# Reordering the segment loop of a recurrent attention kernel on TensorE: half-0 scores ahead of V, the last V bank between the PV halves, one Wo chunk behind PV half 1

## The chip, the cores and the metric

The kernel runs on 1 core of a Trainium2 chip. The metric is the device time of one execution in microseconds (us), as the median of several executions. "Timed" means these executions; "traced" means the one execution of a kernel that the profile was taken from. Engines are named as in the profile: PE is TensorE's matmuls, PEld its weight loads, DVE is VectorE, ACT is ScalarE, POOL is GpSimd.

## The reference

The work is a gated sum of two attention blocks. Block B (a linear-memory attention over four long segments) is the first quarter of the kernel's time and is not touched. Block A is a recurrence over 64 short segments, and it is what this case is about:

```python
for s in range(n_seg):                         # 64 segments of 32 tokens, 8 memory tokens
    h = jnp.concatenate([mem, xs], axis=1)     # 40 rows, 512 wide
    q = jnp.einsum('btd,dhe->bhte', h, Wq)     # 32 heads of 128
    k = jnp.einsum('btd,dhe->bhte', h, Wk)
    v = jnp.einsum('btd,dhe->bhte', h, Wv)
    scores = jnp.einsum('bhqe,bhke->bhqk', q, k) * scale
    p = _softmax(jnp.where(mask[None, None], scores, -1000000000.0), axis=-1)
    o = jnp.einsum('bhqk,bhke->bhqe', p, v)
    o = jnp.einsum('bhte,hed->btd', o, Wo)
    mem = o[:, :M, :].copy()                   # the next segment needs this
    outs.append(o[:, M:, :])
```

Each segment's memory rows come out of the segment before, so segments run strictly one after the other. Inside a segment, V needs only `h`; it does not depend on the softmax.

## The kernel before

A small planner records operations per engine in program order and puts semaphore waits between engines from read and write sets. In the traces of before and after, PE, ACT and DVE run their operations in that order in all 61 segments that start after 380 us (but for one matmul record of PE in before, which stands ahead of three of the scores), so **the order of the Python calls is the order of each engine's queue**. Heads are handled in two halves (0 and 1) for everything from the scores on. Per segment:

```python
def vproj(j):                      # one PSUM bank of V: 8 matmuls 128x512, then its eviction
    P.op("pe", f_v, ..., name="v%d_%d" % (s, j))
    if j in (1, 2):
        P.op("act", ...)           # banks 1 and 2 are evicted by ACT
    else:
        P.op("dve", ...)           # banks 0 and 3 by DVE
# ... cut: scores (32 small matmuls), softmax_exp (exp on ACT, mask on DVE) ...
def softmax_norm(i):
    P.op("pe", ...)                # row sums: one matmul with ones
    P.op("act", ... ACT.Ln)        # ln of the sums
    P.op("act", ... ACT.Exp, scale=-1.0)   # exp(-ln) = inverse
    P.op("dve", ... ALU.mult)      # normalised P
def pv(i):                         # 16 matmuls, then evicted by ACT (one group) and DVE (the other)
    ...
def wo(i, c):                      # 16 weight-load and matmul pairs 128x40: half i, output chunk c
    ...

kq("K", 0); kq("K", 1); kq("K", 2)     # 128 pairs 128x40 (cut: output tail of every fourth segment)
kq("Q", 0); kq("Q", 1); kq("Q", 2)     # 128 pairs 128x40
vproj(0)
scores(0, 16)
scores(16, 32)
softmax_exp(0)
softmax_exp(1)
vproj(1)
softmax_norm(0)
vproj(2)
softmax_norm(1)
vproj(3)
pv(0)
pv(1)
for c in range(C):                     # C = 4
    wo(0, c)
wo(1, 0); wo(1, 1)                     # cut: memory and output copies (tail)
wo(1, 2); wo(1, 3)
```

The softmax here doesn't subtract the row's maximum and nothing guards it: scores larger than these inputs give would overflow.

## Time and profile before

| | before |
|---|---|
| timed, median of 4 (range) | 1468.8 us (1467.2 to 1472.1) |
| traced | 1482.0 us, span 1480.2 us |
| segment phase, first to last Wo stage, 63 periods | 1108.4 us, 17.59 us each |
| shortest period without / with an output tail | 16.50 / 17.58 us |
| stretches at half clock in that phase | 35, together 120 us |

A segment's *period* here is the distance between the starts of two Wo stages in the timeline. Every fourth segment carries an output tail, about 1.1 us. The shortest period of each kind I call the *floor*: it is what the schedule costs when nothing disturbs it.

The page of before: the busy times of the engines, the granted PE clock in 40 slices (9 is 90% or more of full), and who is on the chain of work that ended last.

```profile
PE 1251.3 (85%) x35605; PEld 980.8 (66%) x35653; DVE 621.3 (42%) x1542; ACT 579.6 (39%) x1280; POOL 106.1 (7%) x212
...
PEclk8978697677999999999999999998999999999998
...
PE 57%; ACT 12%; DVE 5%; issue 2%; SPq 1%; DMA 1%
```

PE is the busiest engine, but 17% of the chain runs on ACT and DVE. The chain of waits of before through one softmax (start us, length us, what) shows where:

```profile
727.24 0.60 ACT V_sb L865
727.84 0.34 ACT R_sb L902
...
730.01 0.49 DVE Pn_sb L906
730.50 0.61 DVE V_sb L868
731.11 0.14 issue
731.25 0.37 PE pb L918 x16
```

ACT evicts V bank 1 (L865) *before* it takes the Ln of half 0 (L902), the same again for half 1 (left out), and PV half 1 (L918) starts only when DVE has evicted V bank 3 (L868). The view of waits of PE over the segment phase, from 380 us on (us in total, times, longest), puts a number on it:

```profile
PE pb L918 <- DVE V_sb L868: 82.9, 63, 1.3
PE pb L840 <- issue: 10.1, 24, 0.8
PE pb L943 <- issue: 4.1, 8, 1.2
```

PE stands idle 1.31 us per segment in front of PV half 1. I call this **the hole**.

What a hole does later is seen in stretches of 1 us of the same trace. The first column is the stretch, then its length, busy time of PE, PEld, DVE, ACT and POOL with instruction counts; the third number from the end is the granted clock.

```profile
1100.00:1101.00 1.00, 0.17 (x14) 0.06 (x6) 0.75 (x2) 0.65 (x2) 0.29 (x1) 1.00 0.00 0
...
1102.00:1103.00 1.00, 1.00 (x44) 1.00 (x43) 0.39 (x1) 0.34 (x1) 0.00 (x0) 1.00 0.00 0
1103.00:1104.00 1.00, 1.00 (x39) 1.00 (x35) 0.00 (x0) 0.00 (x0) 0.00 (x0) 0.60 0.09 16
1104.00:1105.00 1.00, 1.00 (x36) 1.00 (x33) 0.12 (x2) 0.00 (x0) 0.00 (x0) 0.50 0.00 0
```

The hole is at 1100.2 to 1101.5; from 1103.2 on PE runs at half clock for 3.41 us, and successive matmuls of Wo and K start 33 ns apart in place of 25.4, although PE is "100% busy" in both. At half clock these pairs thus run at about three quarters of their rate (25.4 of 33 ns), not at half. A Wo stage that holds a whole such stretch takes 4.2 us in place of 3.4. This is why PE's busy share alone would have hidden the second cost.

The third thing to see is the "issue" gap. The timeline of PE of before (start us, length us, engine, line, operation, count, and in brackets the idle time and what ended it):

```profile
1421.47 0.76 PE L943 MATMUL pb<-OT_sb,Wo_sb 128*128 128x40 bf16 x24 [0.73 <-issue]
...
1425.38 0.77 PE L840 MATMUL pb<-hT,Wk_sb 128*128 128x40 bf16 x24 [0.55 <-issue]
...
1429.13 0.77 PE L840 MATMUL pb<-hT,Wq_sb 128*128 128x40 bf16 x24 [0.38 <-issue]
```

Each time exactly 24 of a group's 128 matmuls are left: the gaps lie 128 weight-load and matmul pairs, 256 instructions, apart.

### The profile page before, as it was taken

The numbers are of one execution on the slowest core, as the hardware profiler recorded it, in microseconds if no ns is written. First come the engines' busy times: TensorE is split into PE (matmuls) and PEld (weight loads), VectorE is DVE, ScalarE is ACT, GpSimd is POOL, SyncE is SP. The second block draws the span as 40 slices with busy tenths as digits, with TensorE's granted clock in tenths as the row PEclk, the third lists the DMA queues.
The fourth block names the chain that finished last, engine by engine and source line by source line (L and its number), as shares of the span: only waits on it lengthen the run. The fifth ranks groups of instructions, "written<-read, shape, count | busy, mean of one in ns | idle before, by whom it ended". The sixth has DMA issues, their size and how long they took to land.

```text
span 1480.2 us, 75277 instructions
## 1 busy us (share of the span) xinstructions
PE 1251.3 (85%) x35605; PEld 980.8 (66%) x35653; DVE 621.3 (42%) x1542; ACT 579.6 (39%) x1280; POOL 106.1 (7%) x212
## 2 busy tenths in 40 slices
PE   4767676766999899998998998989998998999988
PEld 3544444445777777776777767777777776777776
DVE  3547676552333334333333434333333343433333
ACT  4757475662333333333333333333333333333333
POOL 1322132220000000000000000000000000000000
PEclk8978697677999999999999999998999999999998
DMA  8000000006000000000000000000000000000000
GB/s 341 3 2 3 2 2 2 2 2 229 4 7 4 7 4 7 4 7 4 7 7 4 7 4 7 4 8 4 7 4 8 4 7 4 7 4 7 4 7 7
DMA packets 12891, 27.90 MB, mean 19 GB/s; under 512 B 800, under 2 KB 11048, under 8 KB 11048
## 3 DMA queue, kind: packets, MB, share of 16 engines
q1 hardware_dynamic: 12584, 23.09, 4.3%
q8 instruction: 280, 4.59, 1.3%
q14 instruction: 27, 0.22, 0.0%
HBM read 20.99 MB, written 2.10 MB: 16 GB/s over the span
## 4 chain that ended last, share of the span: by engine, by line
PE 57%; ACT 12%; DVE 5%; issue 2%; SPq 1%; DMA 1%
PE pb L840 28%; PE pb L943 17%; PE pb L859 8%; ACT V_sb L865 5%; ACT R_sb L904 4%; ACT R_sb L902 3%; DVE V_sb L868 3%; DVE Pn_sb L906 2%; PE pb L885 2%; PE pb L918 2%; PE pb L1008 1%; DMA Wo_sb<-in_A_Wo_dram 1%; SPq L310 1%; PE pb L1016 0%; SPq L304 0%
## 5 line engine op out<-in xcount | busy, mean ns | idle before, releaser
L859 PE MATMUL pb<-Wv_sb,hT 128*40 128x512 bf16 x2048 | 268.2, 383 | 2.0 <-DMA Wv_sb<-in_A_Wv_dram 2.0
L943 PE MATMUL pb<-OT_sb,Wo_sb 128*128 128x40 bf16 x8192 | 244.6, 188 | 9.4 <-issue 4.1
L847 ACT ACTIVATE KT_sb<-pb 128x480 bf16<-128x480 f32 (+1 forms) x192 | 100.9, 526 | 383.4 <-PE pb L840 383.4
L943 PEld LDWEIGHTS pb<-OT_sb,Wo_sb 128*128 128x128 bf16 x8192 | 238.3, 101 | 15.3 <-issue 8.7
L850 DVE CAST QT_sb<-pb 128x480 bf16<-128x480 f32 (+1 forms) x192 | 115.6, 602 | 298.1 <-PE pb L840 291.0
L840 PE MATMUL pb<-hT,Wk_sb 128*128 128x40 bf16 x8192 | 224.5, 181 | 7.8 <-issue 5.0
L840 PE MATMUL pb<-hT,Wq_sb 128*128 128x40 bf16 x8192 | 220.2, 180 | 7.5 <-issue 6.8
L840 PEld LDWEIGHTS pb<-hT,Wk_sb 128*128 128x128 bf16 x8192 | 217.4, 97 | 9.2 <-issue 9.0
L840 PEld LDWEIGHTS pb<-hT,Wq_sb 128*128 128x128 bf16 x8192 | 212.3, 96 | 10.0 <-issue 9.5
L593 ACT ACTIVATE PT_g<-pb 128x512 bf16<-128x512 f32 (+1 forms) x384 | 170.2, 529 | 59.7 <-PE pb L584 58.9
L892 ACT ACTIVATE P_sb<-pb 104x320 bf16<-104x320 f32 x128 | 49.0, 434 | 271.5 <-PE pb L885 271.5
L859 PEld LDWEIGHTS pb<-Wv_sb,hT 128*40 128x40 bf16 x2048 | 85.2, 99 | 81.2 <-issue 3.5
L906 DVE TENSOR_TENSOR Pn_sb<-P_sb,R_sb 104x320 bf16<-104x320 bf16 x128 | 63.0, 492 | 140.6 <-ACT R_sb L904 140.6
L918 PE MATMUL pb<-Pn_sb,V_sb 40*128 40x40 bf16 x2048 | 47.6, 178 | 84.1 <-DVE V_sb L868 84.1
L918 PEld LDWEIGHTS pb<-Pn_sb,V_sb 40*128 40x128 bf16 x2048 | 36.0, 93 | 116.0 <-ACT OT_sb L927 89.0
L988 DVE CAST hT<-pb 128x16 bf16<-128x16 f32 x126 | 22.0, 174 | 199.5 <-PE pb L943 199.5
L868 DVE CAST V_sb<-pb 104x512 bf16<-104x512 f32 x128 | 88.0, 687 | 33.5 <-PE pb L859 33.5
L599 POOL TENSOR_SCALAR_AFFINE_SELECT PT_g<-PT_g 128x512 bf16<-128x512 bf16 x128 | 82.3, 643 | 241.9 <-ACT PT_g L593 239.7
L799 POOL COPY hT<-xT 128x128 bf16<-128x128 bf16 x64 | 19.0, 298 | 1077.6 <-PE pb L859 1060.3
L584 PE MATMUL pb<-QTg,KTg 16*128 16x128 bf16 x1280 | 43.1, 245 | 52.8 <-ACT PT_g L593 49.6
L927 ACT ACTIVATE OT_sb<-pb 128x320 bf16<-128x320 f32 x128 | 56.0, 437 | 79.8 <-PE pb L918 79.7
L865 ACT ACTIVATE V_sb<-pb 104x512 bf16<-104x512 f32 x128 | 75.3, 588 | 17.5 <-PE pb L859 17.4
(92 smaller groups left out, 1026.2 us busy)
## 6 DMA issues: line engine op xcount, KB each, us to landing
Wk_sb<-in_A_Wk_dram SPq DMA_DIRECT2D x4, 1024.0 KB, 11.6
Wq_sb<-in_A_Wq_dram SPq DMA_DIRECT2D x4, 1024.0 KB, 20.8
Wv_sb<-in_A_Wv_dram SPq DMA_DIRECT2D x4, 1024.0 KB, 9.2
Wo_sb<-in_A_Wo_dram SPq DMA_DIRECT2D x4, 1024.0 KB, 14.3
x_sb<-in_A_x_dram SPq DMA_DIRECT2D x4, 512.0 KB, 5.6
out_dram<-fin SPq DMA_DIRECT2D x16, 128.0 KB, 1.9
wqN_sb<-in_B_wq_dram SPq DMA_DIRECT2D x1, 512.0 KB, 7.3
wkN_sb<-in_B_wk_dram SPq DMA_DIRECT2D x1, 512.0 KB, 8.4
```

Source lines behind the costliest of these rows:

```text
L593: P.op("act", (lambda j=j: (lambda a: a.activation(ptb[:, j, 128 * n0:128 * (n0 + len(wv))], pb[j][:, 0:128 * len(wv)], ACT.Exp, scale=SCA ...
L599: P.op("gp", (lambda n=n: (lambda gq: gq.affine_select(ptb[:, :, 128 * n:128 * (n + 1)], ptb[:, :, 128 * n:128 * (n + 1)], [[0, 4], [1, 128]],
L840: ins = pe.matmul(pb[bnk][:, (p - h0) * L:(p - h0 + 1) * L], wsb[:, c, h * E:(h + 1) * E], hTc[:, c, :], start=(c == 0 and (p == h0 or not ...
L847: P.op("act", lambda a: a.activation(dst[:, h0 * L:h1 * L], pb[bnk][:, 0:(h1 - h0) * L], ACT.Copy), reads=[rbank[bnk]], writes=[rd], name= ...
L850: P.op("dve", lambda dv: dv.tensor_copy(dst[:, h0 * L:h1 * L], pb[bnk][:, 0:(h1 - h0) * L]), reads=[rbank[bnk]], writes=[rd], name="Qev%d_ ...
L859: ins = pe.matmul(pb[j][64 * g2:64 * g2 + L, 0:512], hTc[:, c, :], Wv_sb[:, c, n0:n0 + 512], start=(c == 0), stop=(c == C - 1))
L865: P.op("act", lambda a: a.activation(V_sb[0:NP, 512 * j:512 * (j + 1)], pb[j][0:NP, 0:512], ACT.Copy), reads=[rbank[j]], writes=[rv], name ...
L868: P.op("dve", lambda dv: dv.tensor_copy(V_sb[0:NP, 512 * j:512 * (j + 1)], pb[j][0:NP, 0:512]), reads=[rbank[j]], writes=[rv], name="vev%d ...
L904: P.op("act", lambda a: a.activation(R_sb[0:NP, i * W:(i + 1) * W], R_sb[0:NP, i * W:(i + 1) * W], ACT.Exp, scale=-1.0), reads=[rr], write ...
L906: P.op("dve", lambda dv: dv.tensor_tensor(Pn_sb[0:NP, i * W:(i + 1) * W], P_sb[0:NP, i * W:(i + 1) * W], R_sb[0:NP, i * W:(i + 1) * W], AL ...
L918: ins = pe.matmul(pb[2 * i + g2][:, (t % HB_) * L:(t % HB_ + 1) * L], V_sb[p0:p0 + L, t * E:(t + 1) * E], Pn_sb[p0:p0 + L, t * L:(t + 1) * L],
L943: ins = pe.matmul(pb[bk][:, (c % 2) * L:(c % 2 + 1) * L], Wo_sb[:, h, c * 128:(c + 1) * 128], OT_sb[:, h * L:(h + 1) * L], start=(first an ...
```

## The change

The intent: bring the softmax of half 0 forward so that V banks 0 and 1 run under it; let ACT take Ln and inverse ahead of its V eviction; and fill the time before PV half 1 with work that does not need it (V bank 3 and three of the four Wo chunks of half 0). One Wo chunk stays behind PV half 1 to cover the eviction of its result. No arithmetic changes.

```diff
-    vproj(0)
     scores(0, 16)
+    softmax_exp(0)
+    v_mm(0)
+    v_ev(0)
     scores(16, 32)
-    softmax_exp(0)
     softmax_exp(1)
-    vproj(1)
-    softmax_norm(0)
-    vproj(2)
-    softmax_norm(1)
-    vproj(3)
+    softmax_sum(0)
+    softmax_ln(0)          # Ln, inverse (ACT); for half 0 also the normalise (DVE)
+    v_mm(1)
+    v_ev(1)
+    softmax_sum(1)
+    softmax_ln(1)
+    v_mm(2)
+    v_ev(2)
     pv(0)
+    v_mm(3)
+    softmax_nrm(1)
+    v_ev(3)
+    for c in range(3):
+        wo(0, c)
     pv(1)
-    for c in range(C):
-        wo(0, c)
+    wo(0, 3)
     wo(1, 0)
     wo(1, 1)
```

(`vproj` is split into `v_mm` on PE and `v_ev`, its eviction, and `softmax_norm` into `softmax_sum`, `softmax_ln` and `softmax_nrm`, with unchanged bodies.)

More of the change, by code (lines that the diff above doesn't have):

```diff
@@ L851, in kq, with v_mm @@
                  reads=[rbank[bnk]], writes=[rd], name="Qev%d_%d" % (s, b))
-    def vproj(j):
+    def v_mm(j):
         def f_v(pe):
@@ L862, in vproj, with v_ev @@
         P.op("pe", f_v, reads=[rx] + rm + [Rs("Wv")], writes=[rbank[j]], name="v%d_%d" % (s, j))
+    def v_ev(j):
         rv = Rs("V_sb%d" % j)
@@ L896, in softmax_exp, with softmax_sum, softmax_ln @@
              reads=[rp, Rs("amask")], writes=[rp], name="msk%d_%d" % (s, i))
-    def softmax_norm(i):
-        rp, rr, rn = Rs("P_sb%d" % i), Rs("R_sb%d" % i), Rs("Pn_sb%d" % i)
+    def softmax_sum(i):
+        rp = Rs("P_sb%d" % i)
         P.op("pe", lambda pe: pe.matmul(pb[4 + i][:, 0:W], onesg[0:NP, :], P_sb[0:NP, i * W:(i + 1) * W], start=True, stop=True),
              reads=[rp, Rs("onesg")], writes=[rbank[4 + i]], name="sum%d_%d" % (s, i))
+    def softmax_ln(i):
+        rr = Rs("R_sb%d" % i)
         P.op("act", lambda a: a.activation(R_sb[0:NP, i * W:(i + 1) * W], pb[4 + i][0:NP, 0:W], ACT.Ln),
@@ L905, in softmax_norm, with softmax_nrm @@
              reads=[rr], writes=[rr], name="rex%d_%d" % (s, i))
+        if i == 0:
+            softmax_nrm(0)
+    def softmax_nrm(i):
+        rp, rr, rn = Rs("P_sb%d" % i), Rs("R_sb%d" % i), Rs("Pn_sb%d" % i)
         P.op("dve", lambda dv: dv.tensor_tensor(Pn_sb[0:NP, i * W:(i + 1) * W], P_sb[0:NP, i * W:(i + 1) * W],
```

## The prediction

> **What bounds it now.** The 64 recurrent segments take about 1110 of the 1480 us of the profiled span (first to last Wo stage in the timeline), about 17.3 us each. PE is busy for 85% of the span on the page, DVE 42%, ACT 39%. The chain of waits leaves PE only in the softmax, for ACT and DVE. In the view of waits PE waits most before the second PV half, for the DVE eviction of V bank 3: 80.2 us in 61 waits, 1.31 us per segment.
>
> A second cost hangs on it. In 1 us windows the segment phase shows about 37 stretches at granted clock 0.50, each about 3.41 us, 126 us in all, always behind the hole. A Wo stage that carries one takes 4.2 us in place of 3.41, so each costs about 0.8 us, 29 us in all. [...] all stretches fall on one 3.41 us grid, whose phase against the hole decides.
>
> Third, PE has gaps released by "issue" inside the long Wo-K-Q run: 32 in the segment phase, 14 us, nearly all in segments at full clock (about 0.37 us each between 566 and 696 us).
>
> **What the change does.** The same matmuls and evictions are reordered, none added. Half-0 scores (0.2 us) run first, so the exp and mask of half 0 run under V bank 0 (0.97 us). ACT gets half 0's Ln and inverse ahead of the V bank 1 eviction. V bank 3 (0.98 us) goes behind PV half 0, Wo chunks 0-2 of half 0 (48 matmuls at 25.4 ns, 1.22 us) ahead of PV half 1, chunk 3 (0.41 us) behind it.
>
> Walking the segment with the trace's durations (exp 0.43, Ln 0.46, inverse 0.47, V eviction 0.58 on ACT and 0.68 on DVE, normalise 0.49, PV eviction 0.44/0.49, hand-over 0.1-0.14 us): PV half 0 finds its operands ready; ACT's half-0 PV eviction ends just as V bank 3 leaves PE, so Wo waits 0-0.2; V bank 3 is evicted about 0.3 us before PV half 1 needs it, so the 1.31 us wait goes; Wo of half 1 waits about 0.22 us for the PV evictions, which chunk 3 (0.41 us) hides only in part; the early scores wait about 0.1 us for Q. Net estimate: 1.31 - 0.5 = 0.8 us per segment, 51 us.
>
> Without a hole over 0.3 us the half-clock stretches should vanish: 29 us more. But at full clock the issue gaps should come in most segments (64 x 0.4, about 26 us in place of 14): 12 us given back.
>
> **Prediction.** 1469 - 51 - 29 + 12 = about 1400 us, range 1378 to 1424. Faster by over 2%: 0.94, within 2%: 0.05, slower: 0.01.
>
> **What would show it.** PE's wait of PV on the V eviction gone; small waits of Wo on the PV evictions, 10-20 us in all; granted clock near 1.00 through the segment phase; period of a segment near 16.2 us; issue gaps roughly doubled.
>
> **What would make it wrong.** If ACT's order (exp 1 ahead of Ln 0, then two V evictions) holds the PV eviction longer, the hole moves to Wo: gain nearer 40 us, the throttle half kept. If issue gaps grow to 0.8 us per segment, the throttle gain is eaten. If they don't grow, 1385.

1469 - 51 - 29 + 12 = 1401, "about 1400". The 29 us are the estimate from the trace of before, 37 stretches of 0.8 us.

## The result

| | before | after |
|---|---|---|
| timed, median of 4 (range) | 1468.8 us (1467.2 to 1472.1) | 1394.8 us (1393.5 to 1397.4) |
| traced span | 1480.2 us | 1391.9 us |
| segment phase in the trace | 1108.4 us | 1022.4 us |
| floor without / with output tail | 16.50 / 17.58 us | 15.67 / 16.76 us |
| half-clock stretches in the segment phase | 35 | 1, at its very start |

The ratio is 0.950 (95% interval 0.947 to 0.952): faster by 5.0%. Ratios are computed as the mean time of one kernel's fast runs over that of the other's fast runs of the same rounds, so they are not quite the ratio of the medians quoted.

The page of after, the same lines:

```profile
PE 1241.5 (89%) x35605; PEld 966.6 (69%) x35653; DVE 627.6 (45%) x1542; ACT 573.4 (41%) x1280; POOL 106.1 (8%) x212
...
PEclk8978788586999999999999999999999999999999
...
PE 70%; DVE 2%; issue 2%; SPq 1%; DMA 1%
```

ACT has left the chain. The chain of waits of after through the same part of a segment:

```profile
699.95 0.97 PE pb L859 x8
700.92 0.30 PE pb L928 x16
701.23 0.97 PE pb L859 x8
702.20 1.32 PE pb L953 x48
703.52 0.32 PE pb L928 x16
703.84 0.02 issue
703.86 0.50 DVE OT_sb L940
704.37 0.14 issue
704.50 1.78 PE pb L953 x64
```

V bank 2, PV half 0, V bank 3, 48 Wo matmuls and PV half 1 follow each other on PE; only the eviction of PV half 1 (L940) still shows. The waits of PE in after:

```profile
PE pb L953 <- DVE OT_sb L940: 10.8, 62, 0.2
PE pb L840 <- issue: 6.0, 15, 0.7
PE pb L887 <- issue: 1.4, 5, 0.4
```

And the clock, for the same 990 us of the segment phase, first before, then after (columns as above):

```profile
380.00:1370.00 990.00, 900.74 (x27250) 729.66 (x27260) 371.27 (x874) 330.27 (x729) 16.73 (x56) 0.95 0.02 6
```

```profile
380.00:1370.00 990.00, 967.11 (x29532) 777.50 (x29544) 408.79 (x947) 352.83 (x793) 17.60 (x60) 1.00 0.02 6
```

The granted clock rises from 0.95 to 1.00, and 8% more matmuls are started in the same time.

**The ledger of the two traces.** The segment phase is 86.0 us shorter. Floors: 48 x (16.50 - 15.67) + 15 x (17.58 - 16.76) = 52 us. The rest, 34 us, is excess over the floor, which falls from 52.7 to 18.8 us. To split the excess I counted two things. Half-clock stretches cost 4.2 - 3.4 = 0.8 us each: 35 x 0.8 = 28 us before, under 1 us after. And supply gaps (the "issue" gaps above; why I call them so is told in the last experiment), counted from the start times in the trace as gaps of over 0.12 us between successive PE instructions of one line inside the long Wo, K and Q runs: 51 gaps with 23.7 us before, 42 gaps with 15.1 us after. The sums, 28 + 23.7 = 52 and about 16, meet the measured excess to within 3 us.

The two traces differ by 88 us and the timed medians by 74. The traced run of before is one of its slower ones (1482 us; in all rounds its runs lie between 1466 and 1483), while after repeats within 1390 to 1397. So the ledger explains the traces. The faster runs of before were not traced, but the record has the granted clock of 29 other runs of before, and so their time at half clock, 2 x (1 - clock) x span (in the traces of before and after the granted clock is 1.00 or 0.50, nothing between): 217 to 293 us, against 278 in the traced run; about 155 of it lies ahead of the segment phase. The slower runs have more of it (correlation 0.76; 0.21 us of time for each us at half clock, where 0.8 us for a stretch of 3.41 would be 0.23). So before's faster runs seem to be those with fewer half-clock stretches; this is a correlation, not an experiment.

### The profile page after: what moved, and what is told of

It is laid out like the page before. It is cut to its first block, busy times and chain, and to the rows that moved or that the text cites. A ratio compares the mean times of both kernels' runs of the same rounds, so it can differ in the third digit from the quotient of the medians.

```text
span 1391.9 us, 75212 instructions
## 1 busy us (share of the span) xinstructions
PE 1241.5 (89%) x35605; PEld 966.6 (69%) x35653; DVE 627.6 (45%) x1542; ACT 573.4 (41%) x1280; POOL 106.1 (8%) x212
## 4 chain that ended last, share of the span: by engine, by line
PE 70%; DVE 2%; issue 2%; SPq 1%; DMA 1%
PE pb L840 29%; PE pb L859 17%; PE pb L953 14%; PE pb L928 3%; PE pb L887 3%; DVE OT_sb L940 2%; PE pb L902 2%; PE pb L1026 1%; DMA Wo_sb<-in_A_Wo_dram 1%; SPq L310 1%; PE pb L1034 0%; SPq L304 0%; DVE t_sb L1041 0%; DVE fin L1045 0%; SPq L155 0%
## 5 line engine op out<-in xcount | busy, mean ns | idle before, releaser
L953 PEld LDWEIGHTS pb<-OT_sb,Wo_sb 128*128 128x128 bf16 x8192 | 221.8, 96 | 50.5 <-ACT OT_sb L937 42.5
L953 PE MATMUL pb<-OT_sb,Wo_sb 128*128 128x40 bf16 x8192 | 240.1, 180 | 16.1 <-DVE OT_sb L940 10.9
L840 PE MATMUL pb<-hT,Wk_sb 128*128 128x40 bf16 x8192 | 220.1, 180 | 4.6 <-POOL hT L799 2.7
L840 PEld LDWEIGHTS pb<-hT,Wk_sb 128*128 128x128 bf16 x8192 | 212.8, 96 | 6.0 <-issue 5.5
L894 ACT ACTIVATE P_sb<-pb 104x320 bf16<-104x320 f32 x128 | 55.9, 437 | 266.1 <-PE pb L887 265.2
L940 DVE CAST OT_sb<-pb 128x320 bf16<-128x320 f32 x128 | 63.0, 492 | 123.7 <-PE pb L928 123.7
L584 PE MATMUL pb<-QTg,KTg 16*128 16x128 bf16 x1280 | 43.5, 247 | 52.7 <-ACT PT_g L593 48.9
L584 PEld LDWEIGHTS pb<-QTg,KTg 16*128 16x128 bf16 x1280 | 24.0, 103 | 80.1 <-ACT PT_g L593 71.9
## 6 DMA issues: line engine op xcount, KB each, us to landing
Wk_sb<-in_A_Wk_dram SPq DMA_DIRECT2D x4, 1024.0 KB, 11.6
Wo_sb<-in_A_Wo_dram SPq DMA_DIRECT2D x4, 1024.0 KB, 14.2
```

The costliest lines, as they stand in the source:

```text
L584: ins = pe.matmul(pb[j][:, 128 * slot:128 * (slot + 1)], KTg[32 * j:32 * j + DH, 128 * kc:128 * kc + 128], QTg[32 * j:32 * j + DH, 128 * q ...
L840: ins = pe.matmul(pb[bnk][:, (p - h0) * L:(p - h0 + 1) * L], wsb[:, c, h * E:(h + 1) * E], hTc[:, c, :], start=(c == 0 and (p == h0 or not ...
L940: P.op("dve", (lambda o0=o0, bk=2 * i + 1: (lambda dv: dv.tensor_copy(OT_sb[:, o0:o0 + W], pb[bk][:, 0:W])))(), reads=[rbank[2 * i + 1]], ...
L953: ins = pe.matmul(pb[bk][:, (c % 2) * L:(c % 2 + 1) * L], Wo_sb[:, h, c * 128:(c + 1) * 128], OT_sb[:, h * L:(h + 1) * L], start=(first an ...
```

## The experiments

In all, 12 kernels were run, all with correct results. Each was traced; the table has what the traces gave. "Before" is that of the same rounds; it varies, and small differences should be read from the ratio. Gaps are the supply gaps as counted above, half clock the number of stretches in the segment phase (one lies at its very start in most kernels).

| kernel | median us | before us | ratio | floor us | half clock | gaps, us |
|---|---|---|---|---|---|---|
| before, first trace | 1468.8 | | | 16.50 | 35 | 51, 23.7 |
| before again (1 run) | 1481.9 | | | 16.50 | 36 | 47, 23.6 |
| hole filled with 8 idle matmuls | 1455.5 | 1475.5 | 0.986 | 16.49 | 1 | 52, 24.5 |
| hole filled with 4 | 1470.6 | 1479.1 | 0.994 | 16.49 | 1 | 78, 37.6 |
| V bank 3 between, alone | 1484.5 | 1472.0 | 1.008 | 16.81 | 13 | 69, 30.0 |
| Wo split, alone | 1519.2 | 1479.1 | 1.027 | 17.22 | 42 | 39, 14.7 |
| early scores and Ln, alone | 1426.6 | 1475.5 | 0.967 | 15.86 | 1 | 72, 37.2 |
| after | 1394.8 | 1468.8 | 0.950 | 15.67 | 1 | 42, 15.1 |
| after again | 1393.3 | 1472.0 | 0.946 | 15.67 | 1 | 40, 13.8 |
| after, Ln late | 1465.8 | 1479.7 | 0.992 | 16.66 | 1 | 50, 24.0 |
| after, scores and Ln late | 1432.9 | 1472.0 | 0.973 | 16.20 | 1 | 58, 21.5 |
| after, no chunk behind | 1416.6 | 1475.5 | 0.960 | 16.07 | 1 | 26, 11.6 |
| after, two chunks behind | 1375.9 | 1472.0 | 0.935 | 15.34 | 1 | 60, 18.5 |
| after, long run broken | 1423.9 | 1479.1 | 0.963 | 16.30 | 0 | 19, 7.2 |

### Before again

No edit.

> The kernel before, unchanged, for a second trace: its profiled execution took 1482 us, its timed ones 1467 to 1472. Expected: near 1469 us. Theory: floor period of a segment 16.50 us, the 1.31 us wait of PV half 1 in every segment, 25 to 40 half-clock stretches of 3.41 us in the segment phase; the excess of the first profile is in more stretches or more issue gaps than here.

Measured: 1481.9 us, floor 16.50 us, 36 stretches, 47 gaps. The floor and the counts repeat, and so does the time of the first traced run. My expectation of 1469 us missed: before has executions around 1480 us as well as around 1469. It follows that both traces show a slower execution of before, and that the timed gain of 74 us is the one to quote.

### The hole filled: is the half clock worth anything?

```diff
     pv(0)
+    # 8 matmuls 128x512 of hT and Wv into bank 6, result never read
+    P.op("pe", f_fill, reads=[rx] + rm + [Rs("Wv")], writes=[rbank[6]])
     pv(1)
```

> The kernel before with eight idle 128x512 matmuls (0.97 us, into a free bank, result unused) issued in the 1.31 us hole. The hole's time stays, only PE's idleness goes. Theory (half clock follows the hole's idleness and costs 0.8 us each): stretches in the segment phase fall from about 35 to about 0 and the time falls by 20 to 28 us, to 1441-1450. Rival (the half clock is worth nothing, since instruction supply takes the time back): 1463-1470.

Measured: 1455.5 us against 1475.5 of before, ratio 0.986 (0.980 to 0.993), a gain of 20 us. PE's wait in front of PV half 1 in this kernel:

```profile
PE pb L918 <- DVE V_sb L868: 21.3, 62, 0.3
```

The floor did not move (16.49), so the hole still costs its time; only PE's idleness in it went, from 1.31 to 0.34 us. The half-clock stretches went with it, 35 to 1, and the granted clock from 380 to 1370 us is 1.00:

```profile
380.00:1370.00 990.00, 953.54 (x28423) 741.11 (x28433) 380.18 (x893) 338.25 (x747) 16.71 (x57) 1.00 0.02 6
```

Useless work made the kernel faster (by 1.4%, clear of the noise), and the fall is at the lower edge of the theory's 20 to 28 us; the absolute range in the expectation was worked out from 1469 us and missed because before ran slower in these rounds. The half clock is therefore a consequence of the hole and is worth 20 us when timed; in the two traces the segment phase shrinks by 25 us, from 1108.4 to 1083.3.

### Half of the fill: no half clock, and a gain given back

```diff
-    # 8 matmuls
+    # 4 matmuls 128x512
```

> The kernel before with four idle 128x512 matmuls (0.49 us) in the hole in place of eight, so about 0.83 us of the hole stay idle. In the first trace no 3.41 us window with under 1.1 us of the hole in it was followed by a half-clock window. Theory [...]: no or few stretches, 1450-1460 us, as with eight matmuls. Rival (the clock falls in proportion to the idle): half the stretches, about 1463 us.

The theory rests on the trace of before, in which, after the start of the phase, every window followed by half clock held 1.15 us of idle PE or more.

Measured: 1 stretch, the one at the start of the phase, so holes of 0.78 us brought no half clock in this kernel, where those of 1.31 us brought 35, and the stretches did not fall in proportion to the idle. The first half of the theory held. But the time is 1470.6 us against 1479.1, ratio 0.994 (0.992 to 0.995), only 9 us better; 1450-1460 missed. The waits show where the rest went:

```profile
PE pb L918 <- DVE V_sb L868: 48.9, 63, 0.8
PE pb L840 <- issue: 14.8, 37, 0.7
PE pb L943 <- issue: 7.2, 14, 1.2
```

The "issue" rows rose from 14.2 us in before to 22.0, and counted by start times the gaps rose from 23.7 to 37.6 us: of some 28 us of half clock, 14 were given back to gaps. With eight fill matmuls nothing was given back (24.5 us). This looks like the mechanism that my prediction feared, seen in one kernel and not in its neighbour. Whether the missing half clock raised the gaps, or the eight PE instructions that the fill adds to each segment and that shift everything behind them, is not shown.

### The early scores and the early Ln, alone

The changed kernel, with V bank 3 ahead of both PV halves and all of Wo behind them, as before:

```diff
     v_mm(2)
     v_ev(2)
-    pv(0)
-    v_mm(3)
     softmax_nrm(1)
+    v_mm(3)
     v_ev(3)
-    for c in range(3):
-        wo(0, c)
+    pv(0)
     pv(1)
-    wo(0, 3)
+    for c in range(C):
+        wo(0, c)
```

> Only the early scores and the earlier Ln and inverse; V bank 3 ahead of both PV halves and all Wo behind them, as before. Walk with the trace's durations: hole of about 0.55 us before PV half 1, floor period 15.95 us against 15.68 after and 16.50 before; [...]. Theory (the early scores are the part that carries the gain): 1405-1418 us. Rival (the filling of the hole by V bank 3 and Wo carries it): 1440 or more.

Measured: floor 15.86 us (walked: 15.95), a wait of 0.58 us per segment in front of PV half 1, no half clock after the start: the schedule behaves as walked. The time, 1426.6 us, lies between the two theories' ranges, because the gaps took 37.2 us in place of the 15 of after. At the floor this part alone carries 16.50 - 15.86 = 0.64 of the 0.83 us.

### V bank 3 between the PV halves, alone

```diff
-    vproj(3)
     pv(0)
+    vproj(3)
     pv(1)
```

> The kernel before with V bank 3 alone moved between the PV halves; nothing else. Walk: PV half 0 then waits about 0.74 us for the half-0 normalise, and PV half 1 about 1.0 us, since V bank 3's eviction comes later (behind the PV eviction on DVE). Theory: floor about 16.95 us, half-clock stretches as many as before or more, 1490-1510 us, slower than before. Rival (V bank 3 in the hole pays by itself): 1420-1450.

Measured: 1484.5 us against 1472.0, ratio 1.008 (1.005 to 1.012). PV half 0 waits 0.68 us for the normalise and PV half 1 0.97 us for V bank 3; floor 16.81 us:

```profile
PE pb L918 <- DVE V_sb L868: 59.8, 62, 1.0
PE pb L918 <- DVE Pn_sb L906: 42.1, 62, 0.7
```

By itself this move is a small loss, and the rival is out. Two details of the expectation missed. The time is below its range. And the half-clock stretches fell to 13: the idle time per segment is larger than in before (1.65 us), but it is cut in two by V bank 3's matmuls, and two holes of 0.68 and 0.97 us bring far fewer stretches than one of 1.31.

The traces show what goes with a stretch. All stretches lie on one grid of 3.41 us windows: in the trace of before the starts of all 56, those of block B among them, fit a step of 3.4133 us to within 1 ns. In before, 46 windows of the segment phase hold the hole, with 1.25 us of idle PE or more, and 34 of them are followed by one at half clock (in these the hole begins by 1.74 us into the window, in the 12 others from 1.77 us on); of the 275 other windows one is. With V bank 3 between, 10 windows hold both holes, 1.5 us or more, and all 10 are followed by one at half clock; of the 312 others two are. These figures give no sharp limit: in the second trace of before and in the Wo split, three windows with 0.7 to 1.1 us of idle were followed by half clock too, while the holes of 0.78 us of the half fill and of 0.92 us of the late Ln (below), one in each segment, brought no stretch after the start of the phase.

### The Wo split, alone

```diff
     pv(0)
+    for c in range(3):
+        wo(0, c)
     pv(1)
-    for c in range(C):
-        wo(0, c)
+    wo(0, 3)
```

> The kernel before with only the Wo chunks moved: chunks 0 to 2 of half 0 ahead of PV half 1, chunk 3 behind. DVE still evicts V bank 3 ahead of the PV eviction, so the first Wo waits for it about 1.6 us, and Wo of half 1 a little as in the changed kernel. Theory (no part but the early scores pays alone): floor about 17.0 us, 30 or more half-clock stretches, 1490-1515 us. Rival (Wo in the hole pays by itself): 1420-1450.

Measured: 1519.2 us against 1479.1, ratio 1.027 (1.025 to 1.029), slower. The first Wo waits up to 1.72 us, because DVE evicts V bank 3 ahead of the PV result that Wo now needs early; 42 stretches at half clock:

```profile
PE pb L943 <- DVE OT_sb L930: 113.2, 93, 1.7
```

The floor (17.22) and the time were each a little over what I had walked; the direction and the counts are the theory's.

### After, with ACT's order undone

```diff
     softmax_sum(0)
-    softmax_ln(0)
     v_mm(1)
     v_ev(1)
+    softmax_ln(0)
     softmax_sum(1)
-    softmax_ln(1)
     v_mm(2)
     v_ev(2)
+    softmax_ln(1)
     pv(0)
```

> The changed kernel with one thing undone: on ACT each Ln and inverse goes behind the V eviction of its turn again (V bank 1, Ln 0, inverse 0, V bank 2, Ln 1, inverse 1). The early scores, V bank 3 between the PV halves and the Wo split stay. In the trace of after, V bank 1's eviction starts 2.71 us after the early scores and holds ACT; Ln 0 then comes 1.3 us later than in the changed kernel, and PV half 0 waits about 0.97 us. Theory (the early scores pay only because ACT takes the Ln ahead of the V eviction): floor about 16.6 us, 1445-1460 us, still no half clock. Rival (the place of the scores on PE is what pays, ACT's order is second): under 1410 us.

Measured: 1465.8 us against 1479.7, ratio 0.992 (0.987 to 0.997). The floor is 16.66 us (walked: 16.6), *above* that of before. The time range missed by 6 us, with before 11 us slower than in the first rounds. In the timeline, ACT and then PE:

```profile
703.97 0.60 ACT L867 ACTIVATE V_sb<-pb 104x512 bf16<-104x512 f32 x1 [0.72 <-PE pb L859]
704.47 0.43 ACT L907 ACTIVATE R_sb<-pb 104x320 f32<-104x320 f32 x1
704.93 0.47 ACT L909 ACTIVATE R_sb<-R_sb 104x320 f32<-104x320 f32 x1
...
706.07 0.37 PE L928 MATMUL pb<-Pn_sb,V_sb 40*128 40x40 bf16 x16 [0.92 <-DVE Pn_sb L916]
```

ACT sits idle 0.72 us waiting for V bank 1 with the row sums of half 0 long ready (their matmul started at 702.65), since the V eviction stands ahead of the Ln in its queue and ACT ran the two in that order. Against after, where the Ln comes first, the normalise of half 0 starts 1.31 us later, counted from V bank 0 (3.94 us in place of 2.63), and PV half 0 waits 0.92 us. Two calls moved on ACT's queue cost at the floor 0.99 us per segment, more than the whole change brought. The title of the change speaks of PE's order; the part without which nothing is gained at the floor is ACT's.

### After, with the scores and the Ln late

```diff
-    scores(0, 16)
-    softmax_exp(0)
     v_mm(0)
     v_ev(0)
+    scores(0, 16)
     scores(16, 32)
+    softmax_exp(0)
     softmax_exp(1)
-    softmax_sum(0)
-    softmax_ln(0)
     v_mm(1)
     v_ev(1)
-    softmax_sum(1)
-    softmax_ln(1)
+    softmax_sum(0)
+    softmax_ln(0)
     v_mm(2)
     v_ev(2)
+    softmax_sum(1)
+    softmax_ln(1)
     pv(0)
```

> The changed kernel without its early scores: V bank 0 first, both scores, both exps, V bank 1 ahead of the Ln, as before; V bank 3 between the PV halves and the split of Wo kept. Walk with the trace's durations: PV half 0 waits about 0.74 us for the normalise of half 0; floor about 16.2 us; [...]. Theory: 1423-1440 us. Rival (the early scores don't matter once V bank 3 and Wo fill the hole): 1393-1400.

There was one stretch, at the start of the phase.

Measured: 1432.9 us, ratio 0.973 (0.969 to 0.977), floor 16.20 us, PV half 0 waits 0.68 us for the normalise: all as expected. V bank 3 and the Wo split together, which were each a loss alone, bring 16.50 - 16.20 = 0.30 us at the floor when both are in. Compared with the run above, early scores with a late Ln (16.66) are worse than late scores with a late Ln (16.20). Late scores with an early Ln were not run, so what the early scores add by themselves, once the Ln is early, is not shown.

### After, with no chunk behind PV half 1

```diff
-    for c in range(3):
+    for c in range(4):
         wo(0, c)
     pv(1)
-    wo(0, 3)
```

> The changed kernel with all four Wo chunks of half 0 ahead of PV half 1, none behind. Theory (chunk 3 hides 0.41 us of the PV evictions): the wait of Wo half 1 grows from 0.17 to about 0.58 us, floor 16.09 us, time 1395+26 = 1415-1424 us, still no half clock. Rival (that chunk's place does not matter, PE work bounds): 1393-1398.

Measured: 1416.6 us, as the theory had it; floor 16.07 us (expected 16.09), wait of Wo half 1 0.68 us:

```profile
PE pb L953 <- DVE OT_sb L940: 42.8, 63, 0.7
```

The chunk behind PV half 1 is worth its own length, 0.40 us per segment.

### After, with two chunks behind: a version that beats both

```diff
-    for c in range(3):
+    for c in range(2):
         wo(0, c)
     pv(1)
+    wo(0, 2)
     wo(0, 3)
```

> The changed kernel with Wo chunks 0 and 1 ahead of PV half 1 and chunks 2 and 3 behind. In the trace of after, V bank 3's eviction ends 0.52 us before PV half 1 starts, so PV half 1 can come 0.41 us earlier nearly without a wait, and the 0.17 us wait of Wo half 1 is covered. Theory: floor 15.50-15.57 us, time 6 to 10 us under the changed kernel of the same rounds. Rival (PV half 1 then waits for V bank 3 as much as it gains): no difference, or slower.

Measured: 1375.9 us against 1393.3 of the changed kernel in the same rounds, and 1472.0 of before: ratio 0.935 (0.932 to 0.938) to before, 1.25% under the changed kernel. The timeline of PE of this kernel:

```profile
711.67 1.04 PE L859 MATMUL pb<-Wv_sb,hT 128*40 128x512 bf16 x8
712.64 0.98 PE L953 MATMUL pb<-OT_sb,Wo_sb 128*128 128x40 bf16 x32
713.56 0.37 PE L928 MATMUL pb<-Pn_sb,V_sb 40*128 40x40 bf16 x16
713.86 1.82 PE L953 MATMUL pb<-OT_sb,Wo_sb 128*128 128x40 bf16 x65
```

No wait is left between V bank 3 and the next K. I had expected 0.10 to 0.17 us at the floor, since the profile of after lists a wait of 0.17 us; it brought 0.33 (21 us over the phase, of which gaps took 4.7 us back; 17 us are left in the time). The reason is in how idle time is measured. The timeline of PE of after has:

```profile
703.75 0.57 PE L953 MATMUL pb<-OT_sb,Wo_sb 128*128 128x40 bf16 x16
704.50 1.78 PE L953 MATMUL pb<-OT_sb,Wo_sb 128*128 128x40 bf16 x64 [0.17 <-DVE OT_sb L940]
```

In after, the 16 matmuls of chunk 3 start at 703.75, 25.4 ns apart, so the last starts at 704.13, and the next at 704.50: PE could have started one 0.34 us earlier. The listed idle time counts from the last matmul's *end*, some 0.18 us after its start. The listed 0.17 us and the 0.33 us gained differ by 0.16 us, about the 0.18 us that the profile gives one matmul.

### After, with the long run broken: what are the "issue" gaps?

```diff
     kq("K", 2)
+    # 4 matmuls 128x512 of hT and Wv into bank 7, result never read
+    P.op("pe", f_brk, reads=[rx] + rm + [Rs("Wv")], writes=[rbank[7]])
     kq("Q", 0)
```

> The changed kernel with four idle 128x512 matmuls (0.48 us, eight instructions with their weight loads) between K and Q, in the middle of the long run of weight-load and matmul pairs. Floor 16.15 us. Theory (the time over the floor is instruction supply that falls behind in an unbroken run of pairs): the mean over the floor falls from 0.36 to under 0.15 us in the segments without an output tail, time 1406-1416 us. Rival (the gaps do not depend on the run): the excess stays 0.36 us, 1421-1428 us.

Measured: 1423.9 us; the time fell into the rival's range. The parts say something else: the floor rose by 0.63 us and not by 0.48 (the four matmuls take 0.55 us up to the first of Q, and the change of shape behind K costs 0.09), which spoils the time, while the gaps fell from 42 with 15.1 us to 19 with 7.2 us, and the mean excess of a segment without an output tail from 0.38 us (0.35 in its second trace) to 0.18 us (expected: under 0.15). So the gaps do depend on the unbroken run, by half, and the rival's "the excess stays 0.36" is out; the theory is held up in part only.

That I call the gaps instruction supply is read from the traces, not from this run. In every one of the 14 traces they lie multiples of 256 PE instructions apart (give or take a missing record). In the traces of before and after they end a nearly constant time after the landing of a 16 KB packet of the queue that the profile calls "instruction": median 1.38 us in before, with 50 of 51 between 1.2 and 1.6 us, and 1.42 us in after. For the gap that ends at 1421.47 in the lines shown above, the packet landed at 1420.07; for that at 1425.38, at 1423.98 (from the times of the packets in the trace). Back-to-back pairs take 25.4 ns (128 pairs in 3.25 us), so 256 PE instructions are used up in 3.25 us, and gaps that follow one another at the steady rate come 3.75 us apart (1425.38 to 1429.13). That PE waits for what the packet brings is my inference from these times; no view of the profile says it.

## Why the prediction came out right, and which step did not

The time, 1394.8 us, is within 5 us of the predicted 1400. The prediction's counts (37 stretches, 80.2 us of waits) differ a little from those used here (35, 82.9 us); nothing below rests on that. Point by point:

1. **The hole, 1.31 us, and its net worth of 0.8 us per segment, 51 us: right.** The wait of PV on the V eviction is gone; the floor fell by 0.83 us, 52 us over the phase. The waits named in its place came nearly as walked: Wo of half 1 waits 0.17 us (predicted 0.22), Wo chunk 0 does not wait. The walk's value lay in following ACT's queue as well as PE's, as the run with the late Ln shows.
2. **Half clock vanishes, 29 us: right in cause and size in the traces.** 35 stretches of 3.41 us became 1, worth 28 us there by the count. The filled hole shows that it is PE's idleness, not the schedule, that brings it; there it was worth 25 us in the traces and 20 when timed.
3. **"At full clock the issue gaps should come in most segments ... 12 us given back": wrong.** This is the term that was mis-sized. I read 14 us off the view of waits and predicted 26. Counted by start times the gaps were 23.7 us before and 15.1 after: 9 us gained, not 12 lost; in the view of waits, 14.2 and 7.7. Two errors: the view counts from the end of the last matmul, so it had missed 10 us of gaps that were already there; and I took the rate of a stretch at full clock with unbroken Wo-K-Q runs as the rate of any schedule at full clock. The half-filled hole may be the case I had in mind (gaps are at 37.6 us once the half clock is gone). In the changed kernel PV half 1 and a wait lie within the Wo stage. That a broken run halves the gaps is measured; that it is the cause of the difference between before and after is only argued, and the kernel with two chunks behind speaks against it as a full account: it has a longer unbroken run than after, yet only 18.5 us of gaps, while the early scores alone have 37.2. What sets the gaps of one schedule against another stays open.
4. **A base that did not belong to the terms.** I took the terms, 51 + 29 - 12, from a trace of 1480 us and subtracted them from timed runs of 1469. From the trace, 1480 - 68 = 1412 would have been predicted for a trace that took 1392. The wrong sign of the gaps (21 us too little gain) and the faster timed base (some 13 us) nearly cancelled. The prediction's own branch for gaps that do not grow, 1385 us, is nearer the truth about the gaps and 10 us off in the time, on the side that the wrong base gives. The prediction's mechanism held in its two large terms; that it came within 5 us is partly luck.

"Busy times" deserve one remark: PE's busy time hardly fell (1251 to 1241 us) though 88 us went, since what was removed was idle time and slow clock. ACT and DVE did the same work as before.

## What to carry to other kernels

In a chain across engines that run their queues in order, as ACT, DVE and PE did here, the order on the *helper* engine can decide as much as that on the busy one: the two calls moved on ACT's queue cost 0.99 us per segment at the floor, where the whole change brought 0.83. So an eviction that waits for a later product must not stand in a queue ahead of a link of the chain. Parts of a reordering may each lose alone and win together (1.008 and 1.027 alone, 0.30 us won at the floor with both in), so walk the whole schedule, all queues, before discarding a part. And price an idle hole on PE at more than its length where the clock falls behind it (here 35 stretches of 0.8 us behind holes of 1.31 us), and price a gain by the trace it was read from.
